# A Hyena convolution feeding a maxout FFN: the convolution's last stage for two tiles at once, in four blocks of 32 columns

## The chip, the core and the metric

The kernel runs on one core of a Trainium2 chip. The metric is the device time of one execution in microseconds. TensorE is called PE (its weight loads PEld), VectorE DVE, ScalarE ACT, GpSimd POOL; SyncE (SP) only issues DMAs.

## The reference

The first block is a long convolution by FFT, gated by `x`, with B = 4 batches, S = 12544 positions and D = 128 channels; the second is a maxout FFN over all B*S tokens with 768 hidden units:

```python
h_filt = (np.maximum(pos_emb @ w1, 0.0) @ w2) * np.exp(-0.01 * pos)[:, None]
y = irfft(rfft(x * v, 2*S) * rfft(h_filt, 2*S), 2*S)[:S]     # along the sequence
a = (x * y).reshape(B * S, D)
h = np.maximum(np.maximum(a @ moe_w1, a @ moe_w2), a @ moe_w3)
out = h @ moe_w_out
```

All is float32.

## The kernel before

**Stages.** A sequence is laid out as 128 x NB with NB = 98, and the transform of length 128 x 90 (`N1 = 90`) is factored. A first part, up to about 300 us, makes the filter's spectrum and the whole convolution of batch 0 up to its last stage. The main loop (line 1254) then runs over 96 tiles, the 32 tiles (`NT`) of each of batches 0, 1 and 2; a tile is 4 of the 128 residues, N = 392 tokens. While it works on batch b's FFN, it makes batch b+1's convolution in between. The last batch's FFN runs in a stage of its own from about 1817 us, with every product of PE in four blocks of 32 columns (`block[0] = 32`, line 1304).

**A tile.** It has six steps (`NF`), `f` = 0 to 5, each called a slot here; slot numbers count within a batch, 6 i + f. In a slot `up` (line 830) makes 128 hidden units: two products with 392 columns into two of the three hps banks that `hbanks` deals out in turn, a relu on ACT (L835) and a max on DVE (L838). `down` (line 841), two slots behind, multiplies them with the output weights; where `f` is 0 it first adds a product with `lin`. `halves_mm` (line 162) cuts a product with 128 output rows into blocks of `block[0]` columns of the weights, 64 in the main loop, that work beside each other. In the trace a product in float32 makes two records for each block.

**The convolution's last stage** turns the 90 values over k1 back into 4 x 98 values for a tile. `t_load` (line 772) loads `zt` from `zd` in DRAM, four DMAs by SP for batches from 1 on, and for every second tile `xT`, the gate of two tiles. `t_sums` (line 795) makes the sum and the difference of the two halves of k1 (parts 0 and 1), each on 90 x 512 values: L804, or L806 with a sign for the later half of the tiles, which is always on DVE. `t_last` (line 811) makes 8 products of 49 columns by 90 rows, into a bank of the cps pool (two pairs of banks, shared with the convolution), and multiplies by the gate on DVE (L825), which gives `g`, the FFN's input. `zt`, `even` and `xT` have two buffers, `gt` three.

**The convolution of the next batch** comes in two phases. The u-phase (slots up to about 52, and from -14) loads x and v, multiplies and cuts them into planes on POOL, turns them by DMA (`u_dma`), joins them on ACT (`u_join`) and multiplies with the first table (`u_two`, L449, 49-row blocks), 13 or 16 times a batch. The g-phase (from `s0`, slot 58 or 59, to 178) has visits of two `g_quarter` (L547, L557) each five slots or so: products in 64x64 blocks. `g_fold` follows in the next slots (ACT L569, DVE L572), then `q_swap` (ACT), `q_re` and `q_im` (DVE L591, L596, POOL L599), `q_unfold` (DVE L603), and three pairs of visits later the second half of the same `g_quarter`. `q_load` (eight DMAs, L520, four slots ahead of a visit), `h_load` (four, L531, one slot ahead) and `t_load` stand in SP's queue in program order; `w_load`, the stores and most loads of `xT` in POOL's.

**The order.** `conv_steps` (line 660) plans the slots of all this for a batch. `start(x)` gives the visits, `units` those of the u-phase. `load` holds an estimate of DVE's load in each slot, and `emptiest` picks the slot with the least. For a tile i, `plan[i]` has three steps: of the two sums of tile i + 1, and of its `t_last`, which is put at step 3, 4 or 2, away from visits. In the main loop (lines 1274 to 1298) a slot is written as: the loads, `up`, the sums, `down`, `t_last`, and then the convolution's steps of the slot, the visit last. Sums are on POOL as long as the tile begins at or before `s0`, then on DVE.

## Time and profile before

| | us |
|---|---|
| median of 3 runs | 2237.83 (2235.44 to 2241.18) |
| profiled execution | 2231.93 |
| its span, first to last instruction | 2230.1 |
| busy: PE / DVE / ACT / POOL | 2209.7 / 1555.8 / 1216.9 / 1164.0 |
| PE's granted clock | 0.999 |
| `t_last` in cps, all PE records (both groups), 97 times | 95.9 + 94.6 busy |
| sums on DVE, mean of one: L804 / L806 | 0.83 and 0.71 / 0.90 and 0.77 |
| sums on POOL, mean of one: L804 | 1.29 and 1.28 |
| `zt` from issue to landing, least / median / most | 2.0 / 4.1 / 10.3 |

A line of the timeline gives the start, the length, the engine, the line, what is written from what, the shape and how many records are merged. The PE shape `128*64 128x392` means weights of 128 rows by 64 columns and 392 columns streamed. Lengths of PE records overlap, so a step's cost is the distance between starts. The lists of waits give the total, the number and the longest. In the table by windows the columns are the stretch, the busy time and the count for PE, PEld, DVE, ACT and POOL, PE's clock, the share of the 16 DMA engines and GB/s.

### The profile page before, as it was taken

How to read it: one execution, taken by the hardware profiler on the slowest of the kernel's cores; microseconds unless marked ns; L12 is line 12 of the kernel's file. 1: busy time of each engine (PE TensorE's matmuls, PEld its weight loads, DVE VectorE, ACT ScalarE, POOL GpSimd, SP SyncE). 2: the span in 40 equal slices, each digit the busy share in tenths (PEclk: the TensorE clock that was granted, in tenths of full speed). 3: DMA queues.
4: the chain of work that ended last, by engine and by line, in shares of the span. 5: the costliest groups of instructions: out<-in, count | busy, mean ns of one | idle time of the engine just before them, and what ended most of it. 6: DMA issues, size and time to landing. Idle time of an engine off the chain costs nothing.

```text
span 2230.1 us, 77908 instructions
## 1 busy us (share of the span) xinstructions
PE 2209.7 (99%) x32015; PEld 1301.2 (58%) x32015; DVE 1555.8 (70%) x3245; ACT 1216.9 (55%) x2223; POOL 1164.0 (52%) x1580
## 2 busy tenths in 40 slices
PE   9999989999999999999999999999999999999999
PEld 8999955555555555555555555545555545666665
DVE  5689966668878766677888866668878754545443
ACT  3688955556666555556666655556666622222222
POOL 1145457634545566634554467635454426666665
PEclk9999999999999999999999999999999999999999
DMA  8778989979999999869999999869999732222221
GB/s 197 183 237 278 304 183 199 184 169 236 246 247 235 231 192 180 174 159 248 237 243 237 223 205 177 175 156 240 243 244 237 205 79 58 58 67 71 64 58 24
DMA packets 491335, 411.66 MB, mean 185 GB/s; under 512 B 289406, under 2 KB 407920, under 8 KB 490979
## 3 DMA queue, kind: packets, MB, share of 16 engines
q1 hardware_dynamic: 443689, 274.50, 56.0%
q0 software_dynamic: 45808, 130.25, 21.5%
q8 instruction: 252, 4.13, 0.8%
q10 hardware_dynamic: 1482, 1.93, 0.4%
q14 instruction: 104, 0.85, 0.1%
HBM read 262.85 MB, written 84.67 MB: 156 GB/s over the span
## 4 chain that ended last, share of the span: by engine, by line
PE 87%; DMA 6%; DVE 3%; SPq 2%; issue 1%; POOL 1%; ACT 0%; DVEq 0%; POOLq 0%; ACTq 0%
PE hps L167 40%; PE ops L167 16%; PE ops L899 6%; PE ps L167 4%; PE cps L167 3%; PE cps L449 3%; PE ps L176 3%; DMA ht<-hd 3%; PE cps L547 2%; PE sps L1133 2%; PE cps L557 2%; PE gps L1115 2%; DMA sq<-spec 2%; DMA wt<-wq_const 1%; SPq L520 1%
## 5 line engine op out<-in xcount | busy, mean ns | idle before, releaser
L167 PE MATMUL hps<-gt,w_sb 128*64 128x392 f32 (+1 forms) x7672 | 1154.3, 494 | 1.8 <-DVE hid L838 1.0
L835 ACT ACTIVATE hid<-hps 128x392 f32<-128x392 f32 x768 | 382.7, 498 | 757.3 <-PE hps L167 740.6
L167 PEld LDWEIGHTS hps<-gt,w_sb 128*64 128x64 f32 (+1 forms) x7672 | 423.1, 126 | 445.8 <-issue 410.0
L838 DVE TENSOR_TENSOR hid<-hid,hps 128x392 f32<-128x392 f32 x768 | 428.6, 558 | 346.1 <-PE hps L167 329.6
L167 PE MATMUL ops<-hid,wo_sb 128*64 128x392 f32 x2304 | 476.8, 492 | 0.0
L599 POOL TENSOR_TENSOR cb<-cb,xs 128x512 f32<-128x512 f32 x135 | 177.9, 1318 | 404.0 <-DVE xs L596 379.8
L167 PEld LDWEIGHTS ops<-hid,wo_sb 128*64 128x64 f32 x2304 | 165.6, 137 | 213.6 <-issue 213.6
L572 DVE TENSOR_TENSOR cb<-cps,eo 128x512 f32<-128x512 f32 (+1 forms) x288 | 175.2, 650 | 72.5 <-ACT eo L569 71.4
L853 POOL DMA_DIRECT2D out_dram<-ot x96 | 76.6, 798 | 232.4 <-ACT ot L851 216.9
L587 ACT ACTIVATE xs<-cb 32x512 f32<-32x512 f32 x270 | 169.5, 628 | 21.1 <-DVE cb L572 12.3
L588 ACT COPY xs<-cb 32x512 f32<-32x512 f32 x270 | 166.3, 616 | 3.2
L603 DVE TENSOR_TENSOR xs<-cb 128x256 f32<-128x256 f32 x270 | 149.0, 599 | 6.2 <-POOL cb L599 6.2
L429 ACT COPY uT<-turned 113x512 uint16<-113x512 uint16 x180 | 125.9, 770 | 0.1
L386 POOL TENSOR_TENSOR ut<-ut 128x392 f32<-128x392 f32 x90 | 93.3, 1037 | 40.7 <-DMA ut<-in_vr_dram 36.0
L167 PEld LDWEIGHTS cps<-f4p,even 90*64 90x64 f32 x1552 | 87.2, 138 | 35.9 <-issue 33.2
L768 POOL DMA_DIRECT2D xT<-in_x_dram x172 | 101.5, 604 | 3.5 <-DVE hid L838 2.5
L471 DVE TENSOR_TENSOR low<-high,cps 128x180 f32<-128x180 f32 x186 | 54.7, 335 | 68.7 <-ACT high L461 68.7
L580 POOL DMA_DIRECT2D zd<-cb x135 | 95.4, 706 | 13.7 <-DVE cb L572 10.9
L924 POOL DMA_DIRECT2D out_dram<-o x120 | 72.7, 612 | 47.1 <-DVE o L917 45.6
L167 PE MATMUL cps<-f4p,zt 90*64 90x49 f32 x1552 | 95.9, 222 | 0.1
L1103 POOL TENSOR_SCALAR minus<-specH 128x128 f32<-128x128 f32 x45 | 34.4, 764 | 117.7 <-PE gps L1115 93.0
L413 POOL COPY planes<-ut 128x392 uint16<-128x392 uint16 x180 | 95.7, 566 | 0.0
(165 smaller groups left out, 3483.5 us busy)
## 6 DMA issues: line engine op xcount, KB each, us to landing
ht<-hd SPq DMA_DIRECT2D x264, 256.0 KB, 7.4
wt<-wq_const POOLq DMA_DIRECT2D x144, 256.0 KB, 5.2
zd<-cb POOLq DMA_DIRECT2D x135, 256.0 KB, 6.5
zt<-zd SPq DMA_DIRECT2D x384, 90.0 KB, 3.7
sq<-spec SPq DMA_DIRECT2D x528, 64.0 KB, 5.7
ut<-in_xr_dram SPq DMA_DIRECT2D x128, 196.0 KB, 4.1
ut<-in_vr_dram SPq DMA_DIRECT2D x128, 196.0 KB, 4.3
wt<-wt_const SPq DMA_DIRECT2D x90, 256.0 KB, 4.8
```

What stands on the lines that cost most here:

```text
L167: nc.tensor.matmul(out[h:h + w], lhsT[:, h:h + w], rhs, start=start, stop=stop, skip_group_check=True)
L413: nc.gpsimd.tensor_copy(w[:, h, :, :, 0:HB], a[:].bitcast(U16).rearrange("p s (m e h) -> p h s e m", e=2, h=2)[:, h])
L429: nc.scalar.copy(uts[u][0:HR, 8 * (u % 2):8 * (u % 2) + 8].rearrange("n s r t -> n (s r t)").bitcast(U16).rearrange("n (s r t h) -> n h s ...
L572: nc.vector.tensor_tensor(out=cb[:, a, lo:hi], in0=ps[:, lo:hi], in1=eo[:, lo:hi], op=op)
L587: nc.scalar.mul(xs[at:at + 32], xt[at + 32:at + 64], -1.0)
L588: nc.scalar.copy(xs[at + 32:at + 64], xt[at:at + 32])
L599: nc.gpsimd.tensor_tensor(out=xts[g], in0=xts[g], in1=xs[:], op=ALU.add)
L603: nc.vector.tensor_tensor(out=ab[:, q], in0=y[:, 0], in1=y[:, 1], op=(ALU.subtract, ALU.add)[q])
L768: eng.dma_start(xT[c * NG:(c + 1) * NG].rearrange("d i p n -> d (i p) n"), x[:, 4 * i:4 * i + 8, c, b, :])
L835: nc.scalar.activation(h[:], pa[:, 0:N], Relu)
L838: nc.vector.tensor_tensor(out=h[:], in0=h[:], in1=pb[:, 0:N], op=ALU.max)
L899: nc.tensor.matmul(ps[32 * q:32 * q + 32, 0:H2], w[:, m:m + 32], rhs[:, H2 * c:H2 * c + H2], start=start, stop=True, skip_group_check=True)
```

## The change

Sums and last stage are planned for two tiles at once. For each odd tile i, `last` is the step from 1 to 5 nearest to 4 that has a visit (any step, if none has), and there tiles i + 1 and i + 2 have their `t_last`, one after the other, directly ahead of the visit. These run in blocks of 32 columns. All `t_last` planned so take their bank from `hbanks`, the FFN's three, in place of cps. The sums of tile i + 1 may stand from three slots ahead of tile i, those of i + 2 from two slots ahead (a step into it for i = 1), up to the slot before `last`; up to `s0` they stand at the first of these. Tile 1, and the next batch's tile 0, stay alone and 64 wide. The loads move too: an even tile i loads tile i + 2 at step 0 and tile i + 3 at step 1 (at step 5 for i = 0), where each tile loaded i + 2 at step 0.

```diff
-        plan = []
-        busy = {start(x): 2 for x in range(NK + LATE)}
-        for x in range(NK + LATE):
-            busy.setdefault(start(x) + 1, 1)
-        for s in units:
-            for k, n in enumerate((1, 3, 9, 2)):
-                busy[s - 1 + k] = max(n, busy.get(s - 1 + k, 0))
+        visits = {start(x) for x in range(NK + LATE)} | set(units)
+        sums, lasts = {}, {}
+
+        def summed(k, lo, hi):
+            for part in range(2):
+                lo = emptiest(range(lo, hi), 0.7) if lo > s0 else lo
+                sums.setdefault(lo, []).append((k, part))
+
         for i in range(NT - 1):
             s = i * NF
-            last = min((3, 4, 2), key=lambda k: busy.get(s + k, 0))
-            load[s + last] += 0.6
-            if s <= s0:
-                plan.append((0, 0, last))
-                continue
-            a = emptiest(range(s, s + 2), 0.7) - s
-            plan.append((a, emptiest(range(s + a, s + max(a + 1, last - 1)), 0.7) - s, last))
-        plan.append((3, 3, 4))
+            if i == 0:
+                lasts[3] = [1]
+                load[3] += 0.6
+                summed(1, 0, 3)
+            elif i % 2:
+                last = min(range(s + 1, s + NF), key=lambda k: (k not in visits, abs(k - s - 4)))
+                lasts[last] = [i + 1, i + 2]
+                load[last] += 1.2
+                for k, first in zip(lasts[last], (s - 3, s - 2 if i > 1 else s + 1)):
+                    summed(k, first, last)
+        s = (NT - 1) * NF
+        sums[s + 3] = [(NT, 0), (NT, 1)]
+        lasts[s + 4] = [NT]
...
-    def t_last(i, bank=None):
+    def t_last(i, bank=None, width=None):
         zt = zts.pop(i)
         ps = bank or state["bank"]()
+        width, block[0] = block[0], width or block[0]
...
                           f4p[:, i[0] > 0 and i[1] >= NT // 2, a, :], s == 0 and a == 0, True)
+        block[0] = width
...
             if i < NT - 2:
-                if f == 0:
+                if i % 2 == 0 and f == (0 if i else 4) + 1:
+                    t_load(*tiles[n + 3])
+                if i % 2 == 0 and f == 0:
                     t_load(*tiles[n + 2])
...
-            for a in range(2):
-                if f == plan[i][a]:
-                    t_sums(tiles[n + 1],
-                           nc.vector if turn_ or i * NF > pairs_from else nc.gpsimd, (a,))
+            for k, part in sums.pop(i * NF + f, ()):
+                t_sums(tiles[n - i + k],
+                       nc.vector if turn_ or i * NF > pairs_from else nc.gpsimd, (part,))
...
-            if f == plan[i][2]:
-                t_last(tiles[n + 1])
+            ks = lasts.pop(i * NF + f, ())
+            for k in ks:
+                t_last(tiles[n - i + k], next(hbanks), 32 if len(ks) > 1 else None)
```

More of the change, by code (lines that the diff above doesn't have):

```diff
@@ L756, in conv_steps @@
             slots.setdefault(s, []).append((fn, args))
-        return slots, plan, s0
+        return slots, sums, lasts, s0
     N = 4 * NB
@@ L1255 @@
         if i == 0:
-            plan, pairs_from = plans[b]
+            sums, lasts, pairs_from = plans[b]
         if n == 0:
```

## The prediction

> **What bounds the kernel now.** I read the page first: busy times and the chain that ended last.

> ```profile
> PE 2209.7 (99%) x32015; PEld 1301.2 (58%) x32015; DVE 1555.8 (70%) x3245; ACT 1216.9 (55%) x2223; POOL 1164.0 (52%) x1580
> ...
> PE 87%; DMA 6%; DVE 3%; SPq 2%; issue 1%; POOL 1%; ACT 0%; DVEq 0%; POOLq 0%; ACTq 0%
> ```

> PE is busy for 99% and is 87% of the chain, so a microsecond taken off PE's own work is worth a microsecond, as long as no wait takes its place. A busy share can hide what a step costs, so next I read PE's waits between 320 and 1815 us, the main loop. These are all of them but one of 1.3 us for `wt`:

> ```profile
> PE cps L547 <- DMA sq<-spec: 1.3, 3, 0.5
> PE cps L557 <- DVE xs L603: 0.5, 2, 0.3
> ```

> So the price of a step on PE is the distance from its start to the next step's start. The timeline of PE in the main loop shows one `t_last`, 64 columns wide, in cps, and one visit of the convolution in 64x64 blocks:

> ```profile
> 910.56 0.83 PE L167 MATMUL ops<-hid,wo_sb 128*64 128x392 f32 x4
> 911.22 0.27 PE L167 MATMUL cps<-f4p,even 90*64 90x49 f32 x4
> ...
> 912.14 1.50 PE L167 MATMUL hps<-gt,w_sb 128*64 128x392 f32 x8
> 913.47 0.83 PE L167 MATMUL ops<-hid,wo_sb 128*64 128x392 f32 x4
> 914.23 1.48 PE L449 MATMUL cps<-f1e,uT 49*64 49x90 f32 x64
> 915.64 1.54 PE L167 MATMUL hps<-gt,w_sb 128*64 128x392 f32 x8
> 917.01 0.83 PE L167 MATMUL ops<-hid,wo_sb 128*64 128x392 f32 x4
> ```

> `t_last` costs 912.14 - 911.22 = 0.92 us, and the `up` behind it 1.33 instead of 1.32: 0.93. The `down` ahead of the visit takes 914.23 - 913.47 = 0.76, where a `down` ahead of another 128-row step takes 0.66 (911.22 - 910.56): going from one blocking to another costs 0.10. Coming back costs 0.05 more (917.01 - 915.64 = 1.37 against 1.32).

> The last batch already runs `t_last` in four blocks of 32, in a stage that is all 32 wide. The lines around its start also show one change from 64 to 32 columns:

> ```profile
> 1817.22 1.49 PE L167 MATMUL ops<-hid,wo_sb 128*64 128x392 f32 x8
> 1818.63 6.79 PE L167 MATMUL hps<-gt,w_sb 128*32 128x392 f32 x80
> ...
> 2008.79 0.29 PE L167 MATMUL last<-f4p,even 90*32 90x49 f32 x8
> ...
> 2009.49 0.49 PE L167 MATMUL hps<-gt,w_sb 128*32 128x392 f32 x1
> ```

> The narrow `t_last` costs 2009.49 - 2008.79 = 0.70 us, though it has twice the records (64 for 32). The change of width costs 1818.63 - 1817.22 - 2 x 0.66 = 0.09.

> **The change, part by part.** The slots follow from the planner's arithmetic. With visits at `start(x)` and `units`, each of the 15 odd tiles of a batch finds a visit among its steps 1 to 5, so all 45 pairs stand ahead of a visit. Tiles 1 and 32 of each plan stay single and 64 wide.

> *Narrow blocks, on PE.* Before, a pair costs 2 x 0.93 = 1.86. After: a change into 32 columns 0.09, two narrow `t_last` 1.41, and 0.03 for weights that can't be fetched ahead (the five `up` from 1818.63 to 1825.24 take 6.61 for 6.58): 1.53. The change into 64x64 was paid before too. That is 0.33 a pair, 45 x 0.33 = -14.8 us. The unknown here is a change directly from 32 columns to 64x64 behind a step of only 49 columns. The rows bound it by 0 (the two blockings share a drain) and by twice 0.10; I take 0.10, the row for every entry into a visit, and keep +-4.5 us for the ends.

> [...] If each record kept the 29 ns it has now (0.92 / 32), the narrow form would cost 1.86, and the sum would be 45 x 2 x 0.94 = +85 us. [...]

> *The FFN's banks.* The pair takes two of three hps banks. After `up(f)` in banks 0 and 1, the pair writes 2 and 0, and `up(f+1)` takes 1 and 2. Bank 0 waits for the relu (0.50 us) of `up(f)`, with a `down` (0.66) and the first `t_last` (0.70) as cover. Bank 2 must be drained by the first product (L825, 0.56 us): the cover is the second `t_last`, the visit (1.4 or 1.9) and half an `up` (0.66), 2.8 us or more. On DVE the two products wait for their `t_last` in order; behind them stand the visit slot's `q_re`, `q_im` (L591, L596), and then the max of the next `up`, which PE gives out some 3.9 us later. I cost this at 0; if the visit did not follow, each pair would pay about 1 us.

> *Sums.* Their number is the same, but they must be done before one place for two tiles. In g-phase slots (77, 78 of the first plan; 137, 138 of the others; 173, 174 of all) two sums stand in each of two neighbouring slots right before the pair: 6 places. DVE's timeline at slots 137 to 139 before the change gives the steps:

> ```profile
> 1173.06 0.55 DVE L838 TENSOR_TENSOR hid<-hid,hps 128x392 f32<-128x392 f32 x1
> 1173.53 0.42 DVE L603 TENSOR_TENSOR xs<-cb 128x256 f32<-128x256 f32 x1
> 1173.87 0.69 DVE L591 TENSOR_TENSOR cb<-cb,ht 128x512 f32<-128x512 f32 x1
> ...
> 1175.08 0.56 DVE L838 TENSOR_TENSOR hid<-hid,hps 128x392 f32<-128x392 f32 x1
> ...
> 1177.95 0.74 DVE L806 SCALAR_TENSOR_TENSOR even<-zt,sign 90x512 f32<-90x512 f32 x1
> 1178.72 0.75 DVE L806 SCALAR_TENSOR_TENSOR zt<-zt,sign 90x512 f32<-90x512 f32 x1
> ```

> Counted from the start of slot 137: max at 1.5 (without the product of slot 136, which goes away), 0.47 to the sums, 2 x 0.77, then 0.34 + 1.21 (L591 and L596), the second max at 5.05, the first tile's second sum ends at 6.27. PE is ready at 1.98 + 1.98 + 1.98 + 0.09 = 6.03: a stall of 0.25 to 0.3. Were max at 1.89, as it is now, it would be 0.7. I take 0.33, 6 x 0.33 = +2 us, ends 0 and 4. Four sums in one visit slot (3.0 us) are covered: PE needs 4.0 us for it.

> *POOL.* In the first part of each batch POOL does the sums, three slots behind the load instead of six. A slot is 2 us there, so 6 us, and `zt` lands 4.1 us (median) after its issue. Behind the sums on POOL stand `u_mul` and the planes, and SP waits for these with the transposes. The joins come two to four slots later: 0, at most +3 in all.

> *Loads.* No DMA is added; eight `zt` loads now come in two neighbouring slots. They wait for the pair's `t_last` two tiles earlier: sooner by some 4 us where the pair stands early, later by some 3 us where it is in its tile's last step. In the tight places SP holds up to eight transfers in flight, and landings follow the issues. Here is SP, and the share of the DMA engines, at such a place (slots 84 to 88, second plan):

> ```profile
> 1025.39 2.10 SPq L785 DMA_DIRECT2D zt<-zd  x4
> 1028.34 7.58 SPq L520 DMA_DIRECT2D sq<-spec  x8
> 1036.03 2.86 SPq L531 DMA_DIRECT2D ht<-hd  x4
> ```

> ```profile
> 1020.00:1060.00 40.00, 39.40 (x472) 20.98 (x470) 31.05 (x58) 25.75 (x46) 18.57 (x25) 1.00 1.00 251
> ```

> With the engines full, PE's saving can't be kept: of the main loop's chain some 200 us are DMA and SP (994 to 1053 and 1091 to 1138 among them), with some 5 pairs in them, +1.7 us. Four more `zt` ahead of a `q_load` cost up to 4 x 0.3 us, ahead of visits 78, 114 and 139, against the earlier start; I take +1, ends -4 (the 0.9 us stalls of the visits at 88 and 124 go) and +12.

> Sum: -14.8 + 2 + 1.7 + 1 = -10.1 us. The profiled execution took 2231.93 (span 2230.1 and 1.8 around it) and would take 2221.8. The median of the three times is 2237.83, 5.9 above it; on that footing I forecast 2227.8.

> **The rivals.**
> *The second zt load comes late (slower).* In slots 64 (first plan), 88 (the two others), 124 and 160 (all), 9 places, the second tile's load stands behind `q_load`'s eight issues. At 88 that means an issue at 1036.0. DVE reaches its sum at 1042.3 (the `up` ends at 1040.3, max 0.47, two sums 1.5), so a landing over 6.3 us stops DVE, and from 1.5 us more PE waits for the max of slot 89. The `zt` median is 4.1, its longest 10.3: 2.5 us a place, 9 x 2.5 = +22, in all +12: 2250. It decides from 1.1 us a place (landing 8.9 us), and from 1.9 the kernel is slower by over 0.3%. For it: the transfers of `ht` issued there land after 6 to 8 us. Against it: landings follow the issue order, and `zt` would stand ahead of `ht`.
> *DMA sets the pace (no change).* Where the share is 0.95 or more (520 to 780, 1020 to 1290, 1530 to 1720), 24 of the 45 pairs would lose 0.33, 7.9 instead of 1.7: -4, 2234. For it: the shares. Against it: the chain there is mostly PE.
> *The change of blocking costs twice.* Another 0.10 at each pair: -5.6, 2232.

> **How the numbers follow.** Two kernels under 0.3% (6.7 us) apart can hardly be told from no change. Forecast 0.55, with a range of its own of 2222 to 2233; DMA or dearer changes 0.22; late loads 0.20; more than the PE sum 0.03. Faster: 0.88 of the forecast and the last, 0.51; slower: late loads and a little of the others, 0.23; same 0.26. The range for 8 in 10 goes from 2219 (PE sum and the stalls of the visits) to 2246, within the late loads.

> **What would show it.** Right: the pair's 90*32 records in hps, 1.41 us from the first to the visit, the `down` ahead of it 0.75; PE waiting for L806 or L804 under 4 us in all; no wait of DVE for `zt`. Wrong: DVE idle until `DMA zt<-zd` in slots 64, 88, 124, 160; visits over 2.0 us long for `sq`; POOL idle for `zt` and ACT for `turned` behind it.

## The result, and the profile after

The change makes the kernel slower: 2366.05 us (2359.75 to 2374.55) against 2238.76 in the runs beside it, a ratio of 1.0574 [1.0549, 1.0599]. All of it lies in the main loop: from its first product to its last it took 1508.6 us in the profile before and 1640.5 after; what follows takes 417.1 us in both (the first part is 1.0 us shorter).

The busy times and the chain that ended last, after:

```profile
PE 2250.7 (95%) x34895; PEld 1325.3 (56%) x34895; DVE 1577.1 (67%) x3239; ACT 1213.1 (51%) x2223; POOL 1167.4 (49%) x1586
...
PE 72%; DMA 10%; DVE 7%; issue 5%; ACT 2%; SPq 2%; POOL 0%; DVEq 0%; ACTq 0%; POOLq 0%
```

PE falls from 99% to 95%, and its busy time rises by 41 us though its work became less. In the chain "issue" has 5% for 1%: time in which an engine waited for nothing that the profile shows. PE's waits in the main loop from 320 us on (total, times, longest) say where; before they came to 3.1 us. Line numbers have moved: the max is L846 here, the sums are L810 and L812, the relu is L843, the product with the gate L833.

```profile
PE cps L557 <- issue: 18.8, 4, 5.7
PE cps L547 <- issue: 17.4, 8, 4.2
PE hps L167 <- DVE hid L846: 13.1, 19, 1.2
PE cps L449 <- issue: 10.4, 5, 2.3
PE hps L167 <- issue: 9.9, 4, 4.1
PE hps L167 <- DVE zt L812: 4.7, 4, 1.3
PE cps L547 <- DMA sq<-spec: 4.7, 4, 1.9
PE cps L547 <- DMA wt<-wq_const: 3.0, 4, 1.0
...
PE hps L167 <- DVE zt L810: 2.2, 2, 1.3
```

The four "issue" rows are 56.5 us, 46.6 of them in the visits (L449, L547, L557), which now stand behind the pairs. The third row is PE at the first `t_last` of a pair, waiting for the max of the slot before. One such place, by PE's timeline: the visit begins right behind the pair and stops in its middle, with operands and weights there:

```profile
490.14 0.76 PE L547 MATMUL cps<-sq,wt 64*64 64x128 f32 x14
...
491.19 0.49 PE L547 MATMUL cps<-sq,wt 64*64 64x128 f32 x10
495.84 0.48 PE L547 MATMUL cps<-sq,wt 64*64 64x128 f32 x2 [4.16 <-issue]
...
497.31 2.88 PE L167 MATMUL hps<-gt,w_sb 128*64 128x392 f32 x8
499.98 1.34 PE L167 MATMUL ops<-hid,wo_sb 128*64 128x392 f32 x4
```

Behind the gap an `up` takes 2.67 us instead of 1.32. The windows of the same place (PE, PEld, DVE, ACT, POOL, then the granted clock and the share of the DMA engines, the packets' times added up over 16 engines, which can pass 1) show why:

```profile
491.70:494.10 2.40, 0.00 (x0) 0.00 (x0) 1.61 (x3) 0.00 (x0) 0.61 (x1) 1.00 1.15 218
494.20:501.00 6.80, 5.16 (x32) 2.62 (x33) 0.69 (x2) 0.97 (x2) 3.96 (x7) 0.50 0.97 234
501.10:505.00 3.90, 3.90 (x26) 1.69 (x24) 2.08 (x4) 2.89 (x6) 0.68 (x1) 1.00 1.06 198
```

PE stops at 491.68 and works again from 495.84; its clock falls to 0.50 at 494.19 and stays there until 501.02, 5.2 us after the work has come back. In the whole profile 93.9 us run at half clock, in 21 stretches of mostly 3.41 or 6.83 us; before, 8.7 us in 2, none of them in the loop. The difference costs up to (93.9 - 8.7) / 2 = 42.6 us (less where PE idles anyway). Not all of it comes from "issue": the stretch at 524.90 us, for one, follows two waits for DVE (0.34 and 1.26 us).

**What PE waits for in "issue".** The page lists a DMA queue that brings instructions (packets, MB, share of the engines), before and then after:

```profile
q8 instruction: 252, 4.13, 0.8%
```

```profile
q8 instruction: 274, 4.49, 0.8%
```

A packet is 4.49 MB / 274 = 16 KB. PE has 2 x 32015 = 64030 matmuls and weight loads before and 69790 after; divided by 252 and 274 that is 254 and 255 a packet, so the queue is PE's, and a packet holds some 256 instructions. Following its packets in the trace beside five of the gaps without a visible reason, the longer ones:

```
PE stops   resumes   next packet starts   lands     from landing to resumption
491.68     495.84    492.70               494.47    1.37
570.50     574.59    571.87               573.13    1.45
681.78     687.52    685.02               686.11    1.41
1101.63    1105.45   1102.87              1103.92   1.53
1135.89    1141.54   1139.19              1140.28   1.26
```

All 18 such gaps of over 0.3 us end 1.26 to 1.68 us after a packet has landed. The packet itself takes 1.0 to 1.8 us; what varies is when it starts: in the nine shorter gaps 0.4 to 1.6 us before PE runs dry, in the nine longer ones 1.0 to 3.3 us after, with the 16 engines at a share of 1.04 to 1.11 from the stop to the packet's start. The place settles that it is the packet: counted over PE's records in the trace (matmuls, weight loads and its few semaphore waits), all 18 stops stand at the same place of a block of 256 (14273 = 55 x 256 + 193 records ahead of the first, 17857 = 69 x 256 + 193 ahead of the second). So do 72 of the 73 such stops in all other profiles. Counted from that place, no packet of the loop, in any profile, starts more than 296 instructions ahead of the first one that it brings, and before the change each landed 3.2 us or more ahead of it. A pair of narrow `t_last` is 128 records and 128 weight loads in 1.5 us, the visit behind it 64 and 64 in 1.4 to 1.9: one and a half packets in 3.5 us, where a slot of the FFN alone uses 24 instructions in 2 us. Below, such a run of many short instructions is called a burst.

### The profile page after: what moved, and what is told of

It is laid out like the page before. It is cut to its first block, busy times and chain, and to the rows that moved or that the text cites. A ratio compares the mean times of both kernels' runs of the same rounds, so it can differ in the third digit from the quotient of the medians.

```text
span 2361.0 us, 83709 instructions
## 1 busy us (share of the span) xinstructions
PE 2250.7 (95%) x34895; PEld 1325.3 (56%) x34895; DVE 1577.1 (67%) x3239; ACT 1213.1 (51%) x2223; POOL 1167.4 (49%) x1586
## 3 DMA queue, kind: packets, MB, share of 16 engines
q8 instruction: 274, 4.49, 0.8%
## 4 chain that ended last, share of the span: by engine, by line
PE 72%; DMA 10%; DVE 7%; issue 5%; ACT 2%; SPq 2%; POOL 0%; DVEq 0%; ACTq 0%; POOLq 0%
PE hps L167 35%; PE ops L167 12%; PE ops L907 6%; PE ps L167 4%; DMA sq<-spec 4%; DMA zt<-zd 3%; PE cps L449 3%; PE ps L176 3%; PE cps L547 2%; PE sps L1141 2%; PE cps L557 2%; PE gps L1123 2%; DVE xs L596 2%; DMA ht<-hd 1%; DMA wt<-wq_const 1%
## 5 line engine op out<-in xcount | busy, mean ns | idle before, releaser
L167 PE MATMUL hps<-gt,w_sb 128*64 128x392 f32 (+1 forms) x7672 | 1173.3, 498 | 10.4 <-issue 3.8
L843 ACT ACTIVATE hid<-hps 128x392 f32<-128x392 f32 x768 | 382.7, 498 | 850.1 <-PE hps L167 820.4
L846 DVE TENSOR_TENSOR hid<-hid,hps 128x392 f32<-128x392 f32 x768 | 428.0, 557 | 435.9 <-PE hps L167 419.7
L167 PEld LDWEIGHTS hps<-gt,w_sb 128*64 128x64 f32 (+1 forms) x7672 | 438.9, 127 | 494.4 <-issue 422.4
L167 PE MATMUL ops<-hid,wo_sb 128*64 128x392 f32 x2304 | 481.4, 494 | 0.0
L167 PEld LDWEIGHTS ops<-hid,wo_sb 128*64 128x64 f32 x2304 | 168.0, 138 | 217.6 <-issue 216.4
L603 DVE TENSOR_TENSOR xs<-cb 128x256 f32<-128x256 f32 x270 | 151.9, 604 | 5.2 <-POOL cb L599 5.2
L547 PE MATMUL cps<-sq,wt 64*64 64x128 f32 x2160 | 111.4, 294 | 25.8 <-issue 17.4
L557 PE MATMUL cps<-xs,wt 64*64 64x128 f32 x2160 | 108.8, 290 | 23.4 <-issue 18.8
L547 PEld LDWEIGHTS cps<-sq,wt 64*64 64x64 f32 x2160 | 81.5, 143 | 55.6 <-issue 41.5
L596 DVE TENSOR_TENSOR xs<-xs,ht 128x512 f32<-128x512 f32 x135 | 108.3, 802 | 0.0
L557 PEld LDWEIGHTS cps<-xs,wt 64*64 64x64 f32 x2160 | 85.8, 145 | 27.3 <-issue 20.2
```

The costliest lines, as they stand in the source:

```text
L167: nc.tensor.matmul(out[h:h + w], lhsT[:, h:h + w], rhs, start=start, stop=stop, skip_group_check=True)
L547: nc.tensor.matmul(ps[64 * a:64 * a + 64, at:at + D], w[64 * r:64 * r + 64, k, a, :], t[64 * r:64 * r + 64, k, :, a], start=(k == 0), stop ...
L557: nc.tensor.matmul(ps[64 * k:64 * k + 64, at:at + D], w[64 * a:64 * a + 64, k, q, :], ab[64 * a:64 * a + 64, q, k, :], start=(g is None an ...
L596: nc.vector.tensor_tensor(out=xs[:], in0=xs[:], in1=hts.pop(g)[:, 1].rearrange("p k q d -> p q k d"), op=ALU.mult)
L603: nc.vector.tensor_tensor(out=ab[:, q], in0=y[:, 0], in1=y[:, 1], op=(ALU.subtract, ALU.add)[q])
L843: nc.scalar.activation(h[:], pa[:, 0:N], Relu)
```

## The experiments

Three theories stood against each other at first. **Supply**: PE's instruction stream runs dry, since its fetches share the engines with the data. **Blocking**: the step from 32 columns directly to 64x64 blocks costs far more than 0.10. **Order**: sums, banks and the planner's altered slots make DVE late.

```
kernel                                       us        ratio to before [95%]
the change                                   2366.05   1.0574 [1.0549, 1.0599]
both of a pair 64 wide (wide)                2286.65   1.0202 [1.0187, 1.0217]
first 64, second 32 wide (half)              2315.64   1.0335 [1.0320, 1.0351]
the change, fewer transfers (less_dma)       2293.41   1.0239 [1.0214, 1.0264]
before, each t_last 32 wide (single32)       2248.95   1.0038 [1.0022, 1.0054]
wide, in a cps tile (wide_cps)               2398.66   1.0721 [1.0697, 1.0744]
wide, old slots of q (wide_oldq)             2275.35   1.0169 [1.0152, 1.0186]
32 wide, away from visits (apart)            2275.92   1.0169 [1.0154, 1.0184]
apart, cps tile, old slots (apart_cps_oldq)  2300.12   1.0275 [1.0259, 1.0290]
apart, old slots (apart_oldq)                2282.35   1.0195 [1.0169, 1.0222]
apart_oldq, second zt later (apart_later)    2283.12   1.0205 [1.0182, 1.0228]
before, fewer transfers (before_less)        2226.10   0.9952 [0.9935, 0.9970]
apart_oldq, fewer transfers (apart_less)     2237.12   1.0006 [0.9993, 1.0019]
```

**Both 64 wide: everything but the narrow blocks.**

```diff
-                t_last(tiles[n - i + k], next(hbanks), 32 if len(ks) > 1 else None)
+                t_last(tiles[n - i + k], next(hbanks))
```

> The pairs stay where the change puts them (ahead of the visits, in the FFN's banks, same sums and loads), but both tiles are 64 columns wide. A (instruction supply: PE's instructions come in fetches of 256, the narrow pair alone is 256 in 1.4 us and the visit 128 more, so PE runs dry behind it): a pair is 128 instructions now, so PE waits for nothing visible (issue) under 10 us instead of 57, the clock comes back to 0.99 or more; what is left are the waits for DVE (some 35 us), and no saving of 14.8: 2255 to 2280. B (the change from 32 columns straight to 64x64 costs microseconds): the same here, since no such change is left. C (the sums and the order on DVE set the pace): 2320 or more.

It gives 79.4 us back: the narrow blocks, meant to save, are most of the loss. Waits without a visible reason fall from 56.5 to 5.6 us, time at half clock from 93.9 to 27.9. PE's waits in its main loop show that what is left is mostly of another kind, behind DVE:

```profile
PE hps L167 <- DVE hid L846: 14.9, 21, 1.2
PE hps L167 <- DVE zt L812: 5.2, 5, 1.3
...
PE hps L167 <- DVE zt L810: 2.8, 3, 1.2
```

**First 64, second 32 wide.** It halves the extra instructions and keeps the step from 32 columns to 64x64 blocks ahead of each visit.

```diff
-                t_last(tiles[n - i + k], next(hbanks), 32 if len(ks) > 1 else None)
+                t_last(tiles[n - i + k], next(hbanks), 32 if k != ks[0] else None)
```

> Of each pair the first tile is 64 wide, the second 32 wide and directly ahead of the visit, so each of the 45 changes from 32 columns to 64x64 is still there, with 192 instructions in the pair instead of 256. A (instruction supply): issue waits fall to under half of 57 us, time 2255 to 2300. B (the change of blocking itself): the waits stay, 50 us or more, time above 2330. C (DVE): 2320 or more.

The time lies between the change and the 64-wide pair, and so do the waits without a visible reason (57, 24, 6 us for 128, 96 and 64 records in a pair) and what half the clock costs beyond before (43, 21, 10 us). Were it the step in blocking, this kernel would have cost as much as the change. That theory falls. The times of this kernel, of the 64-wide pair and of the next one lie 3 to 16 us above what the supply theory gave; the waits that it named came out as it said.

**The change with fewer transfers.** `ht`, 1 MB for each two groups, is loaded into its two buffers once and then kept; all later loads of it are left out, with them the filter's values for those planes.

```diff
-        ht = hh.tile([P, 2, 2, 2, 2, D], FP32, tag="h", name="ht")
-        for a in range(2):
+        made = len(kept) == 2
+        ht = kept[g // 2 % 2] if made else hh.tile([P, 2, 2, 2, 2, D], FP32, tag="h", name="ht")
+        if not made:
+            kept.append(ht)
+        for a in range(0 if made else 2):
```

> The changed kernel without the loads of ht after the first two (so the filter's spectrum is wrong from there on): a third of the DMA bytes of the visits' phase is gone, all instructions of PE stay. A, if a fetch is late because it stands behind data in the DMA engines: issue waits in the visits' phase fall to under 15 us, clock 0.99, 2290 or less. A, if the fetch has a delay of its own: they stay at 30 us or more. B: they stay. C: DVE's order is the same, so its waits stay, 2320 or more.

PE's instructions are those of the change to the last one, and 72.6 us are gone. PE's waits in its main loop (L552 and L562 are L547 and L557 here, L851 the max):

```profile
PE hps L167 <- DVE hid L851: 13.7, 19, 1.2
PE cps L449 <- issue: 9.5, 5, 2.4
PE cps L552 <- issue: 5.4, 6, 1.7
...
PE cps L562 <- issue: 4.2, 5, 1.3
```

In the visits of the g-phase, where the share of the engines is 0.56 to 0.61 for 0.81 to 0.86 in the change, waits without a visible reason fall from 36.2 us (L547 and L557) to 9.6; in the u-phase, where the transfers are as before, they stay (L449: 10.4 and 9.5). So it is the transfers that delay the fetches, but they are not all: in ten of these visits PE still stopped for 0.4 to 1.7 us, with a packet that had started 1.0 to 2.0 us ahead of the stop. A burst of 384 outruns its packet by about a microsecond even there (9.6 / 10); with the shares of the change it is 3.6 us on average. DVE's part stays too, 13.7 us for the max.

**Before, with each single `t_last` 32 wide** in its old place and bank.

```diff
-                t_last(tiles[n + 1])
+                t_last(tiles[n + 1], width=32)
```

> The kernel before with every last stage of the main loop 32 wide, in its old place and bank, alone: 128 instructions in 0.7 us and two more changes of blocking. A: no waits for issue, as 128 is below a fetch; by the rows 0.93 becomes 0.70 + 0.09 + 0.09 + 0.03, 96 times -0.02, so 2235 to 2239, the same as before within 0.3%. B: a change from 32 columns back to 128x64 could cost as much as the one into 64x64, 100 us or more slower. C: the same as before.

This has more packets of instructions than the change (276) and is only 10 us slower than the kernel before: with 128 instructions at once, in a slot without a visit, PE rarely runs dry (6.5 us without a visible reason in 6 places, where none was expected). The number of instructions alone is not the cause; the burst is. It gained nothing on PE either, since each has the change of width to pay: 0.84 from its first record to the next step and 0.10 ahead of it, against 0.92.

**Wide, in the two halves of a cps tile:** are the waits for the max the rotation of the FFN's banks?

```diff
+            spare = state["bank"]() if ks else None
-            for k in ks:
-                t_last(tiles[n - i + k], next(hbanks))
+            for j, k in enumerate(ks):
+                t_last(tiles[n - i + k], spare[:, 512 * j:512 * j + 512])
```

> Both last stages of a pair 64 wide, directly ahead of the visit as in the change, but in the two halves of one of the convolution's PSUM tiles in place of two of the FFN's banks. Against the 64-wide pair in the FFN's banks (2286.7). Bank theory: the 14.3 us that PE waits there for the maximum of the slot before (20 places) is the rotation of three FFN banks, which the visit covered before; here they fall below 4 us, and the time is 2265 to 2275. Late-VectorE theory (the moved multiplications of the convolution make the maximum late, whoever waits for it): the wait passes to the FFN's next first product, 10 us or more stay, and the time is 2280 to 2288.

The waits for the max go, but the experiment brought a wait of its own: the second `t_last` waits for the first one's product with the gate, because both halves are one tile (86.6 us, 44 times, at L833). By the order of the code an extra turn also falls between a product of the u-phase (slot 2) and its last use (slots 3 and 4), so part of the convolution is overwritten. It tells nothing on its question. The same holds for the kernel that joins this tile with the two edits below:

> All three undone but the narrow blocks: 32-wide pairs, in slots without a visit, in one of the convolution's PSUM tiles, and the convolution's multiplications in their old slots. If supply, banks and VectorE's order are the three causes, and the narrow blocks save the 14.8 us of the forecast, the time is 2225 to 2240. If the supply runs dry on a pair by itself, 2270 or more, with PE idle for no visible reason over 20 us.

It has 36.1 us of that wait; its 2300.12 is not evidence for or against the three causes.

**Wide, with the multiplications back in their old slots.** The change enters sums and last stages into `load` differently, and `emptiest` then gives `q_re`, `q_im` and `q_unfold` other slots. DVE's and POOL's timeline after shows what that does:

```profile
1096.15 0.68 DVE L591 TENSOR_TENSOR cb<-cb,ht 128x512 f32<-128x512 f32 x1
1096.38 1.59 POOL L599 TENSOR_TENSOR cb<-cb,xs 128x512 f32<-128x512 f32 x1 [4.15 <-DVE xs L596]
1096.75 1.76 DVE L596 TENSOR_TENSOR xs<-xs,ht 128x512 f32<-128x512 f32 x1
...
1098.44 0.55 DVE L846 TENSOR_TENSOR hid<-hid,hps 128x392 f32<-128x392 f32 x1
...
1099.05 0.29 PE L167 MATMUL hps<-f4p,even 90*32 90x49 f32 x8 [0.95 <-DVE hid L846]
```

Two groups' multiplications stand in a row; the second L596 runs beside the first one's addition on POOL and takes 1.76 us instead of 0.68, the max comes behind it, and the pair's first bank is the one that this max frees. Of the 19 waits for the max after, 15 (11.6 of 13.1 us) stand behind such a long L596; the kernel before has none of these. The edit keeps two lists, the old one for the convolution's steps:

```diff
+        own = load[:]
...
-                lo = emptiest(range(lo, hi), 0.7) if lo > s0 else lo
+                lo = emptiest(range(lo, hi), 0.7, own) if lo > s0 else lo
...
-                load[last] += 1.2
+                own[last] += 1.2
...
+            load[s + last] += 0.6
+            if s <= s0:
+                continue
+            a = emptiest(range(s, s + 2), 0.7) - s
+            emptiest(range(s + a, s + max(a + 1, last - 1)), 0.7)
```

> Both last stages of a pair 64 wide in the FFN's banks as in the 64-wide pair run before (2286.7), and the convolution's multiplications, additions and unfoldings (q_re, q_im, q_unfold) back in the slots that they have in the kernel before: their own list of loads is kept, the sums and last stages are entered in another. Late-VectorE theory: no multiplication runs 1.7 us beside GpSimd's addition any more, the 14.3 us of waits for the maximum fall below 5, and the time is 2268 to 2276. Bank theory: the waits stay above 10 us and the time is 2282 to 2290.

L596 (total and mean), wide and then with the old slots, and there the wait for the max (now L862):

```profile
L596 DVE TENSOR_TENSOR xs<-xs,ht 128x512 f32<-128x512 f32 x135 | 110.1, 816 | 0.0
```

```profile
L596 DVE TENSOR_TENSOR xs<-xs,ht 128x512 f32<-128x512 f32 x135 | 92.0, 681 | 0.0
```

```profile
PE hps L167 <- DVE hid L862: 5.0, 12, 0.6
```

The mean is back at the 681 ns of the kernel before, the wait for the max falls from 14.9 to 5.0 us in the same banks, and the time by 11.3. The late-VectorE theory holds for two thirds of that wait; the rotation alone would have kept it. What is left was not followed: this kernel is still 38 us slower than the kernel before, with 30.8 us of waits in the loop, among them 7.1 for the sums, 6.7 for `wt` (3.0 in wide) and 6.5 for the relu that frees a bank of the FFN (4.2 in wide), which may be the rotation's.

**The change with its pairs away from visits.**

```diff
-                last = min(range(s + 1, s + NF), key=lambda k: (k not in visits, abs(k - s - 4)))
+                last = min(range(s + 1, s + NF), key=lambda k: (k in visits, k - 1 in visits, abs(k - s - 4)))
```

> The change with its 32-wide pairs in the FFN's banks, but each pair placed in a slot that holds no visit of the convolution (and follows none where there is a choice): the burst of 256 short instructions stands without the visit's 128 behind it and without the change to a 64x64 product of the convolution. Theory of the instruction supply: PE's stream is asked for some 300 instructions ahead, so 256 alone is borderline and 384 runs dry: idle time without a visible reason falls from 57 us to below 25, time at half clock to below 40 us of 94, and the whole is 2285 to 2310. If a burst of 256 runs dry by itself, or the transfers load the DMA engines alike everywhere, it stays at 2340 or more. Bank theory adds: without a visit behind it the wait for the maximum merely moves to the FFN's next product, so some 10 us stay.

With as many instructions as the change (274 packets) the waits without a visible reason fall to 7.9 us, and the time by 90 us, to below the 2285 to 2310 that was expected. Here a burst of 256 mostly gets through; in the change one of 384, with 56.5 us of such waits, often did not. PE's waits in this kernel's loop:

```profile
PE cps L547 <- DMA sq<-spec: 10.8, 11, 2.0
PE hps L167 <- DVE hid L846: 10.7, 9, 1.5
PE cps L547 <- DMA wt<-wq_const: 4.8, 5, 1.5
PE cps L449 <- issue: 3.3, 1, 3.3
```

As the bank theory added, the wait for the max moved to the FFN's next product, at 10.7 us. Two causes seemed to be left, to be undone one after the other: the late max, by the old slots, and the late `sq` and `wt`, by a later second load.

> 32-wide pairs in the FFN's banks, in slots without a visit, and the convolution's multiplications, additions and unfoldings in the slots of the kernel before. If the supply (cured by the place) and the late VectorE (cured by the old slots) are two causes that add, the 10.7 us that PE waits for the maximum in the kernel with the pairs apart (2275.9) fall below 4 us, half-clock time falls with them, and the time is 2258 to 2268. If the waits for the maximum are the bank rotation's, they stay near 10 us and the time is 2272 to 2280.

PE's waits with the pairs apart and the multiplications in their old slots:

```profile
PE cps L547 <- DMA sq<-spec: 7.9, 8, 1.5
PE cps L547 <- issue: 7.5, 5, 2.3
PE cps L547 <- DMA wt<-wq_const: 7.1, 8, 1.9
PE cps L449 <- issue: 5.4, 3, 3.6
...
PE hps L167 <- DVE hid L862: 1.0, 2, 0.5
```

The wait for the max went, from 10.7 to 1.0 us, and nothing was won: 2282.35 for an expected 2258 to 2268, a little more than its twin. The waits without a visible reason grew from 7.9 to 17.0 us and those for `sq`, `wt` and `ht` from 15.6 to 17.6; the time at half clock did not fall either (29.2 and 33.0 us). The causes do not add. The second load was moved all the same:

```diff
-                if i % 2 == 0 and f == (0 if i else 4) + 1:
+                if i % 2 == 0 and f == (3 if i else 5):
...
-                for k, first in zip(lasts[last], (s - 3, s - 2 if i > 1 else s + 1)):
+                for k, first in zip(lasts[last], (s - 3, s if i > 1 else s + 1)):
```

> As the 32-wide pairs apart with the multiplications in their old slots, and the second tile's load (zt) issued two slots later, at slot 3 of the even tile in place of slot 1, with its sums placed from two slots later on. If the two loads in a row on SyncE's queue are what makes the convolution's inputs late (sq 10.8 us and wt 4.8 us of waits with the pairs apart, 1.3 and 1.3 before), these waits fall to below 8 us together and the time lies 6 to 10 us below its twin, at 2250 to 2260. If the transfers are late because the DMA engines are full and not because of the order in the queue, the waits stay at 13 us or more and the two times agree within 4 us.

PE's waits with the second load later, the longest four:

```profile
PE ops L167 <- issue: 8.0, 3, 3.7
PE cps L547 <- issue: 6.6, 3, 3.3
PE cps L557 <- issue: 6.4, 2, 3.4
PE cps L547 <- DMA sq<-spec: 4.0, 6, 0.8
```

Both expectations came true in the waits they named and failed in the time. The waits for `sq` and `wt` did fall, to 4.8 us, so the place of that load was their cause, though not by the order in SP's queue alone, as `wt` stands in POOL's. And the time stayed, while the waits without a visible reason rose to 23 us. Each wait that was taken away came back as another, as if something behind them set the pace. Each list is of one execution, and executions of one of these kernels differ by 5 to 11 us, so the single shifts are rough. The last two runs test that it is the DMA engines, with the same loads of `ht` left out as above, in the kernel before and in the pairs apart:

> The kernel before, with the filter tile ht of 1 MB loaded from memory only for its first two buffers and kept from then on (the later loads are left out, and with them the filter's values for those planes). It is the yardstick for the next kernel: PE bounds it with 4 us of idle time in the loop, so it should run within 6 us of the kernel before, at 2231 to 2238. If the transfers paced it unseen, 2225 or less.

> The 32-wide pairs apart, with the multiplications in their old slots (2282.4), and the same loads of ht left out. If what is left there (PE idle 17 us without a visible reason and 18 us for sq, wt and ht, and 16.5 us lost at half clock) is a full set of DMA engines that delays instructions and data alike, so that what one wait gives up another takes, nearly all of it goes: idle without a visible reason below 6 us, the waits for sq and wt below 5, and the time 2225 to 2245. If the narrow pair runs the supply dry by its own length, whatever the transfers do, the idle time without a visible reason stays at 12 us or more, and the time at 2262 or more.

The windows from 560 to 800 us, with the share of the engines next to last: the pairs apart with the old slots, and then with fewer transfers.

```profile
560.00:800.00 240.00, 233.83 (x3135) 118.01 (x3124) 186.15 (x331) 146.04 (x264) 117.28 (x153) 0.99 0.92 229
```

```profile
560.00:800.00 240.00, 239.66 (x3144) 119.62 (x3144) 187.31 (x343) 152.34 (x276) 121.47 (x164) 1.00 0.66 170
```

With the share at 0.66 the pairs apart win 45.2 us, and PE's idle time in the loop falls from 36.9 to 7.1. The kernel before wins only some 10 from the same loads (a little more than expected: even there the transfers cost something), so 35 us are what these transfers cost this version and not the old one. The loads left out also stood in SP's queue; what part of the 35 us is that queue's, and not the engines', was not separated. Even so this version wins nothing: 2237.12 against 2226.10. Of these 11 us 6.6 are idle time (7.1 against 0.5); the rest is not assigned.

No version that computes the whole beats the kernel before.

## Why the prediction was wrong

The forecast was 2227.8 us in 2219 to 2246, faster; the time is 2366.05, outside the range and on the other side.

- *What bounds the kernel: right, and not enough.* PE was the bound. But in the windows of the main loop the DMA engines had a share of 0.93 to 1.00 as well (1.00 from 560 to 800 us), and the prediction used that only to let 1.7 us of a gain lapse. Both were full; a change that loads either had no slack to draw on.
- *Narrow blocks on PE, -14.8: the step that failed.* Its price for the work is right: from a pair's first record to the visit's it is 1.59 us (median; 1.54 at the least), for 1.41 + 0.10 in the prediction, and 2.00 where the pair is 64 wide, for 1.86 + 0.10. Less 0.10 for the change of width ahead that is 0.31 a pair, where 0.33 was forecast. The step from 32 columns to 64x64 so takes 1.54 - 1.41 = 0.13 at the least; that the two blockings share a drain, the prediction's lower end of 0, was not shown. What it left out, and so put at nothing, is that 64 records more in a pair are 128 instructions more, and that these must arrive. The narrow blocks as a whole cost +79.4 us, not -14.8: some 51 us of waits without a visible reason (56.5 against 5.6) and up to 33 us of half clock (93.9 against 27.9 us, halved), with the saving of 14 against them. That is 70 of the 75.4 us between the two profiled spans; the other 5 are not assigned. The rows it took its price from were the last batch, at 1817 to 2230 us: there the DMA engines move at most 71 GB/s by the slices of the page before, in the loop mostly 160 to 250. The row was right about PE's work and silent about its supply.
- *The +85 us, at 29 ns a record.* The prediction worked this out for the case that each record kept the 29 ns it had; the last batch, with 0.70 / 64 = 11 ns, spoke against it. The narrow blocks' 79.4 us happen to be near it. The mechanism is another: a record in the pairs takes 1.59 / 128 = 12 ns, as the row had said, and the loss depends on the other transfers (72.6 us of it go in less_dma) and on what follows the burst (90 go in apart).
- *The FFN's banks, 0: wrong, 13.1 us of waits for the max.* It looked at the relu of the same slot and at the products of the pair itself. It did not ask for the max of the slot before, which frees the first bank of the pair. That max is late because the change also moves L591 and L596, which the prediction left where they were: it followed the planner's arithmetic for sums and last stages, but not what `emptiest` does with the multiplications afterwards. Undoing that alone, in the 64-wide pair, brought 11.3 us.
- *Sums, +2 with ends 0 and 4: too small.* The six places are right: PE waits there for L810 or L812 after, but 6.9 us in all, about 1.15 us a place where 0.33 was taken; DVE was later than counted.
- *Loads, +1.7 and +1.* `sq` and `wt` cost 7.7 us for 2.6 before: +5.1, inside the ends of -4 and +12. POOL at 0 is right: no wait of PE in the loop is put down to it.
- *The rivals.* DVE waits for a late `zt` 2.2 us in 3 places, so the slower rival did not happen. "DMA sets the pace" had the right resource and the wrong price: it foresaw that a gain would lapse, 2234, not that PE would run dry and lose its clock on top.
- *The sum, from the profiles:* 56.5 of waits without a visible reason, (36.7 - 3.1) of others, 42.6 of clock at most, -14 of saving, is 119 of the 131 us by which the span grew. The remaining 12 are not assigned.

What is shown: that PE stops where a packet of its instructions ends, that the narrow blocks make the larger part of the loss (wide), that it grows with the instructions in the burst (half), that it depends on the transfers beside it (less_dma, apart_less) and on the place (apart); and that the multiplications' slots make the max late (wide_oldq). What stays open: why a packet starts late, as the trace shows when it starts and not when PE asked for it; and the 38 us by which even wide pairs with the old slots are slower than the kernel before.

## What to carry to other kernels

Before cutting a step into more and shorter instructions, count them over the few microseconds around it, with the next step's, and set that against the packets of the instruction queue and the share of the DMA engines there; a price taken from a stage with lightly loaded DMA engines (here at most 71 GB/s) said nothing about the supply in one where they moved 160 to 250. With PE busy for 97% and the DMA engines at 0.92 (apart_oldq, 560 to 800 us), a wait that was taken away came back as another until the transfers became fewer: look for the resource, not for the longest wait. And when a planner's estimates are edited, list every step that reads them, not only those that the change is about.
